# Placing every operation of a fused attention and feed-forward kernel with a list scheduler, and moving its turns from TensorE to the DMA crossbar

## The chip, the cores and the metric

The kernel runs on one core of a Trainium2 chip. The metric is the device time of one execution in microseconds (us), measured on the chip. Lower is better. The kernel before takes 428.44 us (median of 2 runs, 428.42 to 428.45).

Names used below: PE is TensorE (matmuls), DVE is VectorE, ACT is ScalarE, POOL is GpSimd, and SP is SyncE, which here only starts DMAs. PSUM is the memory that TensorE writes. To "turn" a tile means to transpose it. A "crossbar DMA" is this document's name for what the traces call DMA_TRANSPOSE: a DMA that transposes on its way.

## The reference

```python
# q, k, v: (8 batches, 8 heads, 576 rows, 64), float32; w_phi: (64, 128)
def phi(x):
    proj = einsum('bhsd,df->bhsf', x, w_phi)
    proj = proj - max(abs(proj), axis=-1, keepdims=True)      # row maximum
    return concatenate([exp(proj), exp(-proj)], axis=-1)
q_p, k_p = phi(q), phi(k)
kv  = einsum('bhsf,bhsd->bhfd', k_p, v)
z   = sum(k_p, axis=2)
num = einsum('bhsf,bhfd->bhsd', q_p, kv)
den = einsum('bhsf,bhf->bhs', q_p, z)[..., None] + 1e-06
x   = num / den                                               # -> (4608 tokens, 512)
out = (relu(x @ w_gate) * (x @ w_val)) @ w_out                # d_ff = 1536
```

Each batch passes through an attention stage (k features, the small matrices kv, q features, numerators and denominators) and then through a feed-forward stage. The feed-forward stage is most of the matmul work.

## The kernel before

Batches are handled as 512 rows in four blocks of 128, and the 64 rows left over are paired ("mixed" tiles). Operations are written by hand into time slots ("ticks"), and that order becomes the fixed order of each engine. k, q and x are turned by matmuls against an identity, and the result is copied from PSUM:

```python
def transposed(blocks):                       # k and q
    for i, blk in enumerate(blocks):
        nc.tensor.matmul(pt[:, P*i : P*i+P], lhsT=blk, rhs=ident, is_transpose=True)
    nc.vector.tensor_copy(t.rearrange("p a b -> p (a b)"), pt[:, 0 : n*P])

def project_rows(T2, m):                      # row-major projection + row maxima
    for i in range(2):
        nc.tensor.matmul(pp[:, 2*F*i : 2*F*(i+1)], lhsT=T2[:, i, :], rhs=w2...)
    nc.vector.tensor_reduce(m, pp..., axis=AX.X, op=ALU.max, apply_absolute_value=True)

def q_rows(st, i):                            # q: rows are projected for the maxima only
    project_rows(...); ...
    nc.scalar.activation(st["c"], st["m"], AF.Exp, scale=2.0)

def q_cols(st, x, slot, lo, par, first):      # q again, feature-major: the features used
    nc.tensor.matmul(pf, lhsT=w2[:, par, :], rhs=st["T"][:, lo : lo+4]...)
    nc.scalar.activation(x["qp"]..., pf, AF.Exp, scale=±1)

def q_finish(x, dst):                         # x is turned for the feed-forward
    for i in range(NDC):
        nc.tensor.matmul(pt[:, P*i : P*i+P], lhsT=x["xu"]..., rhs=ident, is_transpose=True)
    nc.vector.tensor_copy(dst, pt...)
# ... (numerators, feed-forward and the hand-written ticks are cut)
```

So q is projected twice: once row-major, to find the maxima, and once feature-major, to make the features. Most loads are on POOL; the loads of v from the third batch on are on SP, with the stores.

## Time and profile before

| | before |
|---|---|
| time, median | 428.44 us |
| span of the profiled run | 426.3 us |
| TensorE busy | 398.7 us (94%) |
| TensorE idle in the first 45 us / after that | 16.5 / 11.2 us |
| granted TensorE clock | 0.998 |

The lines below are from the page of the kernel before. The first gives busy time by engine; the others cut the span into 40 slices: each digit is a busy share in tenths, and PEclk is the TensorE clock that was granted, in tenths.

```profile
PE 398.7 (94%) x3357; PEld 232.9 (55%) x3416; DVE 284.1 (67%) x641; ACT 250.9 (59%) x575; POOL 159.6 (37%) x204
...
PE   3777899989999999999999999999999999999995
...
PEclk9999999999999999999999999999999999999999
DMA  8997795245413750167015901374020002002004
```

From the sixth slice to the last but one TensorE is full (9, once 8). The trace's records of the clock begin at 18.4 us and show the full clock until 424.6 us, after the last matmul. Before 18.4 us, 256-column projections start 214 ns apart, and 109 ns apart later: the start runs at about half speed, though the digits show it as 9. The next lines are the table by stretches of the same kernel; the columns are the stretch, its length, the busy us of each engine with its instruction count, the granted clock, the DMA share and GB/s.

```profile
core 0: us, PE busy (x) PEld busy (x) DVE busy (x) ACT busy (x) POOL busy (x), PEclk, DMA share, GB/s
90.00:135.00 45.00, 43.60 (x396) 26.06 (x402) 33.17 (x72) 30.10 (x71) 21.14 (x27) 1.00 0.38 74
135.00:180.00 45.00, 44.20 (x387) 26.12 (x395) 35.77 (x85) 28.57 (x66) 16.59 (x22) 1.00 0.41 74
...
270.00:315.00 45.00, 44.58 (x399) 26.41 (x405) 32.12 (x70) 30.80 (x73) 23.13 (x31) 1.00 0.40 80
```

In each 45 us of the middle TensorE is idle for 0.4 to 1.4 us. Nothing but less TensorE work, or a shorter start, can help much. Three groups of the same page show the work in question (line, engine, operation, output and input, count, busy us and mean ns, then the idle time before and its cause):

```profile
L147 DVE TENSOR_REDUCE mk<-pa 128x4 f32<-128x512 f32 x72 | 48.4, 682 | 11.3 <-PE pa L142 11.1
...
L299 PE MATMUL pa<-ident,xu 128*128 128x128 bf16 x144 | 14.0, 219 | 2.1 <-POOL xu L292 1.6
...
L305 DVE COPY xT<-pa 128x512 bf16<-128x512 bf16 x32 | 13.3, 417 | 1.9 <-PE pa L299 1.7
```

The reduction takes 682 ns, a turn of a 128x128 block of x 219 ns by its pipelined record. Last, the waits of SP's queue in the kernel before (total us, times, longest us):

```profile
SPq L355 <- ACT out_sb L352: 325.2, 31, 34.3
```

SP waits almost only for what it stores (this line, and 27.0 us at the last stores); 40 us more it stood before loads of v. Only stores and loads of v are on this queue.

### The profile page before, as it was taken

What the parts mean: (1) busy time and instruction counts of PE and PEld (TensorE: products, weight loads), DVE (VectorE), ACT (ScalarE), POOL (GpSimd) and SP (SyncE); (2) the same over time, 40 slices, a digit from 0 to 9 for tenths busy, and PEclk for the clock granted to TensorE, in tenths of its full rate; (3) what the DMA queues carried; (4) which work ended last, traced back from release to release, by engine and by line L of the source; (5) the groups of instructions that cost most, each with busy time, mean ns of one, the idle gap of its engine ahead of it and who ended that gap; (6) DMA issues with size and microseconds to landing.
All of it is one profiled execution on the core that took longest, in us unless ns stands there. A gap on an engine that the chain in (4) does not pass through costs nothing.

```text
span 426.3 us, 8695 instructions
## 1 busy us (share of the span) xinstructions
PE 398.7 (94%) x3357; PEld 232.9 (55%) x3416; DVE 284.1 (67%) x641; ACT 250.9 (59%) x575; POOL 159.6 (37%) x204
## 2 busy tenths in 40 slices
PE   3777899989999999999999999999999999999995
PEld 1556665645556556555566556555565554444442
DVE  4888569867687679866876699676856795330420
ACT  3984776566667755687567665766667552322321
POOL 8953861176217501574155211870362021000000
PEclk9999999999999999999999999999999999999999
DMA  8997795245413750167015901374020002002004
GB/s 157 199 265 164 108 181 61 75 122 59 56 51 98 128 61 2 61 156 94 2 59 160 116 3 52 71 139 51 26 76 2 1 14 86 2 0 100 0 2 98
DMA packets 45337, 33.66 MB, mean 79 GB/s; under 512 B 12848, under 2 KB 40112, under 8 KB 45296
## 3 DMA queue, kind: packets, MB, share of 16 engines
q0 software_dynamic: 30480, 16.52, 28.1%
q1 hardware_dynamic: 14816, 16.58, 12.4%
q8 instruction: 27, 0.44, 0.4%
q14 instruction: 14, 0.11, 0.1%
HBM read 37.81 MB, written 9.44 MB: 111 GB/s over the span
## 4 chain that ended last, share of the span: by engine, by line
PE 78%; DVE 10%; ACT 4%; POOL 2%; issue 2%; DMA 2%; POOLq 0%; DVEq 0%; ACTq 0%
PE pf L320 40%; PE pf L342 17%; PE pa L142 6%; PE pa L218 5%; PE pa L263 4%; PE pa L241 3%; PE pa L131 3%; DVE u L287 2%; DVE mk L147 2%; DMA qn_117<-in_q_dram 2%; DVE t L279 2%; PE pa L299 1%; POOL xu L292 1%; ACT qp L247 1%; ACT t L275 1%
## 5 line engine op out<-in xcount | busy, mean ns | idle before, releaser
L320 PE MATMUL pf<-xT,wv_sb 128*128 128x512 bf16 (+1 forms) x386 | 96.9, 366 | 3.8 <-DVE xT L305 2.6
L320 PE MATMUL pf<-xT,wg_sb 128*128 128x512 bf16 (+1 forms) x394 | 97.7, 366 | 2.0 <-ACT val_sb L329 1.4
L292 POOL TENSOR_TENSOR xu<-u,r 128x512 bf16<-128x512 f32 x36 | 37.5, 1042 | 164.1 <-DVE r L290 128.9
L329 ACT CAST val_sb<-pf 128x512 bf16<-128x512 f32 (+1 forms) x114 | 65.3, 573 | 52.7 <-PE pf L320 52.3
L247 ACT ACTIVATE qp<-pa 128x512 bf16<-128x512 f32 x128 | 69.5, 604 | 11.9 <-PE pa L241 11.9
L320 PEld LDWEIGHTS <-wg_sb 128*128 128x128 bf16 x456 | 44.4, 98 | 41.6 <-issue 2.1
L320 PEld LDWEIGHTS <-wv_sb 128*128 128x128 bf16 x456 | 43.3, 98 | 36.5 <-issue 3.9
L147 DVE TENSOR_REDUCE mk<-pa 128x4 f32<-128x512 f32 x72 | 48.4, 682 | 11.3 <-PE pa L142 11.1
L263 PEld LDWEIGHTS <-qp 128*128 128x128 bf16 x640 | 33.9, 98 | 21.5 <-issue 0.9
L287 DVE TENSOR_TENSOR u<-pa,t 128x195 f32<-128x195 f32 (+3 forms) x120 | 40.5, 338 | 6.8 <-ACT t L275 0.5
L279 DVE TENSOR_TENSOR t<-pa,cq 128x195 f32<-128x195 f32 (+3 forms) x114 | 37.6, 330 | 4.6 <-PE pa L263 3.8
L352 ACT COPY out_sb<-pf 128x512 f32<-128x512 f32 x36 | 21.3, 592 | 32.4 <-PE pf L342 29.5
L263 PE MATMUL pa<-kv,qp 128*128 128x65 bf16 x640 | 37.9, 193 | 0.9 <-DVE u L287 0.5
L331 DVE SCALAR_TENSOR_TENSOR h_6277<-pf,val_sb 128x512 bf16<-128x512 f32 x12 | 8.3, 692 | 22.8 <-PE pf L320 22.8
L331 DVE SCALAR_TENSOR_TENSOR h_6056<-pf,val_sb 128x512 bf16<-128x512 f32 x12 | 8.3, 692 | 14.5 <-PE pf L320 14.5
L299 PEld LDWEIGHTS <-xu 128*128 128x128 bf16 x144 | 10.7, 98 | 11.7 <-POOL xu L292 3.8
L223 ACT CAST kv<-pa 128x260 bf16<-128x260 f32 x28 | 10.7, 380 | 10.0 <-PE pa L218 9.9
L299 PE MATMUL pa<-ident,xu 128*128 128x128 bf16 x144 | 14.0, 219 | 2.1 <-POOL xu L292 1.6
L331 DVE SCALAR_TENSOR_TENSOR h_566<-pf,val_sb 128x256 bf16<-128x256 f32 (+1 forms) x18 | 9.1, 506 | 8.8 <-ACT val_sb L329 4.1
L331 DVE SCALAR_TENSOR_TENSOR h_1578<-pf,val_sb 128x512 bf16<-128x512 f32 x12 | 8.3, 691 | 9.6 <-ACT val_sb L329 5.7
L305 DVE COPY xT<-pa 128x512 bf16<-128x512 bf16 x32 | 13.3, 417 | 1.9 <-PE pa L299 1.7
L331 DVE SCALAR_TENSOR_TENSOR h_3132<-pf,val_sb 128x512 bf16<-128x512 f32 x12 | 8.2, 686 | 7.3 <-PE pf L320 3.8
(580 smaller groups left out, 776.1 us busy)
## 6 DMA issues: line engine op xcount, KB each, us to landing
out_dram<-out_sb SPq DMA_DIRECT2D x32, 256.0 KB, 2.3
wv_sb<-in_moe_w_val_dram POOLq DMA_DIRECT2D x3, 512.0 KB, 8.2
wg_sb<-in_moe_w_gate_dram POOLq DMA_DIRECT2D x3, 512.0 KB, 9.7
wo_sb<-in_moe_w_out_dram POOLq DMA_DIRECT2D x1, 1536.0 KB, 13.3
vn_1018<-in_v_dram SPq DMA_DIRECT2D x1, 1024.0 KB, 8.9
vn_335<-in_v_dram POOLq DMA_DIRECT2D x1, 1024.0 KB, 13.5
vn_1793<-in_v_dram SPq DMA_DIRECT2D x1, 1024.0 KB, 7.1
vn_2508<-in_v_dram SPq DMA_DIRECT2D x1, 1024.0 KB, 7.2
```

What stands on the lines that cost most here:

```text
L142: nc.tensor.matmul(pp[:, 2 * F * i : 2 * F * (i + 1)], lhsT=T2[:, i, :], rhs=w2.rearrange("p a f -> p (a f)"),)
L147: nc.vector.tensor_reduce(m, pp.rearrange("p (c f) -> p c f", f=F), axis=AX.X, op=ALU.max, apply_absolute_value=True,)
L247: nc.scalar.activation(x["qp"][:, s, slot].rearrange("p a b -> p (a b)"), pf, AF.Exp, scale=sign)
L263: nc.tensor.matmul(pn[:, E * (2 * i + s) : E * (2 * i + s + 1)], lhsT=x["qp"][:, s, slot, blk, :], rhs=kvs[b, h // 2][:, h % 2, s, :],)
L279: nc.vector.tensor_tensor(t, ab[:, :, 1], st["c"][rows, col(lo) : col(lo + n - 1) + 1 : col(1) - col(0)][:, :, None].to_broadcast([np_, n, ...
L287: nc.vector.tensor_tensor(x["u"][rows, lo : lo + n], ab[:, :, 0], t, op=ALU.add)
L292: nc.gpsimd.tensor_tensor(x["xu"], x["u"][:, :, 0:D], r.to_broadcast([P, 8, D]), op=ALU.mult)
L299: nc.tensor.matmul(pt[:, P * i : P * i + P], lhsT=x["xu"][:, 2 * i : 2 * i + 2].rearrange("p a d -> p (a d)"), rhs=ident, is_transpose=True,)
L320: nc.tensor.matmul(ps, lhsT=w[:, dc, P * fi : P * fi + P], rhs=xT[:, dc, lo:hi], start=(dc == 0), stop=(dc == NDC - 1),)
L329: nc.scalar.copy(st["val"], ps)
L331: nc.vector.scalar_tensor_tensor(st["h2"][:, fi, lo:hi], ps, 0.0, st["val"], op0=ALU.max, op1=ALU.mult)
L342: nc.tensor.matmul(st["po"], lhsT=st["h2"][:, fi, P * t : P * t + P], rhs=wo_sb[:, fi, :], start=(fi == 0), stop=(fi == NFC - 1),)
```

## The change

The intent is to take the turns and q's row-wise projection off the busiest engine:

1. Every operation becomes an object with an engine, an estimated duration, its dependences and its buffers. A list scheduler simulates the engines at build time and takes the ready operation with the smallest key. The resulting order is fixed in the program.
2. After the first batch, k, q and x are turned by crossbar DMAs, all issued by SP.
3. q's row maxima come from the feature-major projections. A transposing reduction gives the maxima of 32x32 blocks; one DMA carries these to DRAM, four DMAs bring them back in another arrangement, and a small reduction finishes ("the trip" below). There are seven such trips, one for each batch after the first, and four smaller ones for the mixed tiles: 11 trips, 55 DMAs. The row-wise projection of q goes.
4. The loads of v move from SP to ACT's queue.

The core of the diff (cut; the scheduler, the buffers and the feed-forward are left out):

```diff
-    def transposed(blocks):
-        ... nc.tensor.matmul(..., rhs=ident, is_transpose=True) ... nc.vector.tensor_copy(...)
+    def turn_dma(src, dst, nbytes, dst_buf, deps, key, src_buf):
+        def go():
+            nc.sync.dma_start_transpose(out=dst(), in_=src())
+        return op(SP, 0.1, go, deps, [src_buf, dst_buf], key=key, kind="a", nbytes=nbytes * 1.6)
...
-    def q_rows(st, i):
-        project_rows(...)
+        def amax():                                    # in q_cols
+            nc.vector.tensor_reduce(dst, ps.t.rearrange("p (h j t) -> p h j t", j=NQ, t=32),
+                axis=AX.X, op=ALU.max, apply_absolute_value=True, apply_transpose=True)
...
+    def q_scale(mq, mg, cq, n, deps, key):             # deps: all eight reductions of a batch
+        def away():
+            nc.sync.dma_start(out=dq.t[:, 0 : NQ * n], in_=mq.t...)        # to DRAM
+        def back():
+            for j in range(NQ):
+                nc.sync.dma_start(out=mg.t[32 * j : 32 * (j + 1)], in_=src[j])
+        def amax(): nc.vector.tensor_reduce(mc.t[:, 0:n], mg.t..., axis=AX.X, op=ALU.max)
+        def ex():   nc.scalar.activation(cq.t, mc.t[:, 0:n], AF.Exp, scale=2.0)
+        a  = op(SP, 0.1, away, deps, [mq, dq], ..., nbytes=P * NQ * n * 4)
+        b_ = op(SP, 0.4, back, [a], [mg, dq], ..., nbytes=P * NQ * n * 16)
...
-        at(t + 20, load_v, b + 1)                      # on SP
+        heads_of(b, "vn", v, nc.scalar, ACT, 0, H, (1, b), [o])
+        got["vm", b] = load_rest_by_head(b, v, nc.scalar, ACT, (1, b), ins[b]["vm"], [o])
...
-    for _, _, fn, args in sorted(events, key=lambda e: e[:2]):
-        fn(*args)
+    order = plan.run(lambda kind, now: 5 if kind == "a" else 4)
+    for o, e in order: ...
```

## The prediction

> **What bounds the kernel now.** TensorE. The page's busy line gives PE 398.7 us of a 426.3 us span (94%), DVE 67%, ACT 59%; the chain of waits is 78% PE. The table by stretches shows PE idle for 16.5 us of the first 45 us, 2.2 us from 45 to 90, 0.4 to 1.4 us in each later 45 us, and 4.9 us in the last 66. The granted clock is 0.99 to 1.00. So only fewer PE instructions, or a shorter start, can pay.
>
> **What goes.** Costs read start to start in the PE timeline (181 to 225 us): a 128x128 turn 56 ns, a 256-column projection 109 ns, a 512-column matmul 216 ns. By the instruction lists:
> - 254 of 288 turns of k and q go (batch 0 keeps its own): 14.2 us.
> - 128 of 144 row-wise projections of q, which served only the row maximum: 14.0 us.
> - 128 of 144 turns of x: 7.2 us.
>
> Sum 35.4 us. The feed-forward has 48 more matmuls but the same columns: about nothing. The same costs summed over all that before issues give 391 us; the other 35 us of its span are idle, cold clock and tails.
>
> **What moves.** DVE loses the copies of turned blocks (16 of 0.69 us, 76 of 0.42 us, a few kept) and gains 23 kv copies (0.43 us), 40 small reciprocals (0.2 us) and 11 small maxima. The 64 transposing reductions read the same 128x512 from PSUM; I estimate the 0.68 us of those they replace. DVE ends near 260 us, ACT near 230. Neither binds.
>
> **What is added.** 71 crossbar DMAs, about 12 MB, in SP's order with the stores. [...] This trace shows no such transpose; it is my weakest input. Each turned tile becomes a chain (POOL product, some 2 to 4 us of DMA, then PE), and q's maxima go through DRAM and back. These latencies lie beside an earlier batch's feed-forward and should mostly be hidden. But the order is fixed at build time: where a DMA lands later than the scheduler assumed, PE waits. I allow 1 us a batch.
>
> **On the critical path.** Nearly all 35.4 us, since PE has almost no idle after 45 us. Batch 0 keeps its PE turns and loads, so the start stays about as long; perhaps 5 us is won by filling it better. 428.4 - 35.4 - 5 + 7 = 395, and the scheduler may keep a little more.
>
> **Predicted: 393 us, 8 in 10 within 381 to 408. Chances: faster by over 2% 0.92, within 2% 0.04, slower 0.04.**
>
> **What would show each step.** PE busy near 363 us; turns gone from the PE groups after batch 0. PE idle after 45 us of 5 to 12 us, mainly released by DMAs on turned tiles. Transposing reduction 0.65 to 0.75 us. Crossbar DMAs of 256 KB landing in 3 to 5 us, mean DMA share 50 to 60%. First 45 us with 11 to 17 us of PE idle.
>
> **What would make it wrong.** Crossbar transposes several times slower (10 us per 256 KB would queue on SP and starve PE: no gain); a transposing reduction of twice the cost, making DVE the limit; SP holding a turn behind a waiting store; or, the other way, a much shorter start, giving under 381.

The mean DMA share of 50 to 60%: before, the queues' shares on the page add up to 41%, and what was to come on top was the estimate; 57% was measured. The times of 2 to 4 us and 3 to 5 us for crossbar DMAs are estimates too, and so are the 10 us per 256 KB; the trace before holds no crossbar DMA (its plain stores of 256 KB landed in 2.3 us, median), and what the kernel after measured is given below: 2.5 us for x's turns of 128 KB, 3.9 us for q's of 256 KB and 8.5 us for k's of 256 KB (medians). The "cold clock" is the start told of above (214 ns against 109 ns).

## More of the kernel before

One more thing matters later: the row maximum of q scales the numerator and the denominator of a row alike, so it cancels except against the 1e-06. It is there to follow the reference and to keep the exponentials in range.

## The result, and the profile after

The changed kernel takes 469.5 us (median of 2 runs, 469.23 to 469.76). Its ratio to the kernel before is 1.096, with a 95% interval of 1.093 to 1.099: it is slower by about 41 us, where 35 us of gain were expected. A ratio is the mean time of one kernel's fast runs over that of the other's in the same rounds, so it is not quite the ratio of the medians quoted.

The page after, the same lines:

```profile
PE 385.3 (82%) x2954; PEld 210.5 (45%) x2954; DVE 261.1 (56%) x644; ACT 237.6 (51%) x503; POOL 155.1 (33%) x179
...
PE   1769599659819594999997799989595999999995
...
PEclk9998899959969798799999899999797999999999
DMA  9999969530981929232097995406946003101004
```

The table by stretches after, the same rows:

```profile
90.00:135.00 45.00, 29.08 (x208) 14.86 (x207) 25.30 (x56) 21.75 (x48) 16.14 (x19) 0.84 0.64 99
135.00:180.00 45.00, 36.79 (x320) 20.13 (x320) 25.05 (x64) 26.79 (x57) 19.03 (x22) 0.85 0.52 86
...
270.00:315.00 45.00, 43.71 (x362) 23.50 (x361) 30.73 (x79) 27.19 (x57) 13.01 (x16) 1.00 0.51 100
```

TensorE is busy for only 29.1 us of the stretch from 90 to 135, and in that stretch its clock is 0.84. Where it isn't starved (270 to 315) it runs as before. So there are two losses. To size them I added up the records of the trace: the union of TensorE's busy intervals, and the part of it that lies in stretches at half clock. Half of the latter is lost, by arithmetic; "work" is the busy time less that half.

| us, profiled run | before | after |
|---|---|---|
| span | 426.3 | 467.3 |
| work at full clock | 398.7 | 364.7 |
| lost at half clock | 0 | 20.5 (half of 41.1) |
| idle, first 45 us | 16.5 | 18.6 |
| idle, later | 11.2 | 63.4 |

The saving of work came as intended (34.0 us). It was eaten by 52 us more of idle time and by 20.5 us of half clock, which before did not have at all in its clock records. (Those begin at 18.4 us before and at 18.6 us after. Busy time that lies earlier, 9.9 and 7.9 us, stands in the table as work, although in both kernels 256-column projections start 213 to 214 ns apart there, about half speed; by these numbers the difference between the kernels is an estimated 1 us.)

The same half clock can be read from single lines, in the chosen stretch of TensorE's timeline after (start, us, engine and line, operation, count, idle before it and its releaser):

```profile
124.05 1.03 PE L719 MATMUL ps<-xT,wv_sb 128*128 128x512 bf16 x4
...
138.15 0.38 PE L521 MATMUL ps<-vs,kp 128*128 128x65 bf16 x4 [11.86 <-ACT qp L567]
...
139.22 1.90 PE L719 MATMUL ps<-xT,wg_sb 128*128 128x512 bf16 x4
```

Four 512-column matmuls take 1.03 us before the gap of 11.86 us and 1.90 us after it. The trace's records of the clock hold 11 stretches at 0.5; they last 3.41, 6.83 or 10.24 us, multiples of 3.41 us (the last one runs past the end). I cut the trace into windows of that length, in step with the clock's changes. The 11 drops follow windows in which TensorE was busy for 0 to 44%; from the first record on, in the windows that kept the full clock it was busy for 48% or more, and the clock came back after windows in which it was busy for 79% or more. So in this trace several short gaps did what one long gap did: in the window before the drop at 158.6 us TensorE was busy for 29%, and no gap was over 1.5 us.

What was TensorE waiting for? The label of the gap says ACT. ACT's timeline in the same stretch:

```profile
121.85 0.38 ACTq L324 DMA_DIRECT2D vn<-in_v_dram  x1
122.35 14.13 ACTq L337 DMA_DIRECT2D vm<-in_v_dram  x2
136.53 2.56 ACT L567 ACTIVATE qp<-ps 128x512 bf16<-128x512 f32 x5 [14.19 <-DMA kT<-kn]
```

ACT did nothing for 14 us: it stood in the issue of the second half of a load ("vm", 64 KB of v), and the features that TensorE needed were behind that issue in ACT's order. SP's timeline in the same stretch:

```profile
121.97 5.35 SPq L397 DMA_TRANSPOSE kT<-kn  x2
127.42 0.53 SPq L583 DMA_DIRECT2D dq<-mq  x1
128.12 1.20 SPq L397 DMA_TRANSPOSE kmT<-km  x1
136.01 1.73 SPq L588 DMA_DIRECT2D mg<-dq  x4
```

SP started two turns of k at 121.97, then sent the maxima of q ("dq") at 127.42, and could issue the way back ("mg") only at 136.01. The out-leg of 64 KB needed 8.6 us beside k's turns.

Why did ACT stand in a load, which needs nothing from SP? The trace's DMA records name the semaphore that each DMA counts up and waits on. The 193 DMAs of SP and ACT share eight such semaphores in rotation, and each of them was issued only after the previous DMA on its semaphore had landed, at the closest 0.08 us after. The held load was started at 135.86; the previous DMA on its semaphore was a turn of k that landed at 135.79. The three other long holds of ACT have the same form, after a turn of k, a DMA of "mg" and one of "dq", each within 0.1 us of that landing. In the whole trace none of the 242 DMAs starts before the previous one on its semaphore has landed. Before, ACT issued no DMA, and no DMA waited in this way (each started at least 3.6 us after the previous one on its semaphore had landed). ACT's holds sum to 33.8 us after.

In this trace it is the issuing engine that stands in such a wait: ACT stood for 12.9 us before the load that was started at 135.86.

The waits of SP's queue after:

```profile
SPq L397 <- POOL xu L678: 76.8, 19, 14.1
SPq L397 <- DMA kn<-in_k_dram: 54.8, 5, 20.5
SPq L583 <- DVE mq L553: 37.6, 3, 18.6
...
SPq L588 <- DMA dq<-mq: 18.7, 6, 6.6
```

SP's order now holds urgent things behind waiting ones. It stood 37.6 us at the door of the trip until q's reductions were done, and 18.7 us until the out-leg had landed; turns and stores stood behind. The two larger waits, of turns for their own inputs, aren't what the trip costs: in e20 below, without the trip, they are 94.8 and 76.7 us. The DMA issues after (KB each where given, median us to landing):

```profile
out_dram<-ob SPq DMA_DIRECT2D x32, 256.0 KB, 2.4
...
dq<-mq SPq DMA_DIRECT2D x7, 64.0 KB, 3.0
mg<-dq SPq DMA_DIRECT2D x28, 16.0 KB, 2.1
xT<-xu SPq DMA_TRANSPOSE x28, 2.5
...
kT<-kn SPq DMA_TRANSPOSE x14, 8.5
qT<-qn SPq DMA_TRANSPOSE x14, 3.9
```

A turn of 256 KB of k takes 8.5 us, a store of the same 256 KB 2.4 us. From the end of the last reduction of a batch to the start of the small final one, the seven trips took 12.1, 19.2, 21.3, 9.4, 6.5, 13.5 and 5.8 us.

Three groups of the page after:

```profile
L719 PE MATMUL ps<-xT,wv_sb 128*128 128x512 bf16 (+1 forms) x432 | 103.7, 377 | 18.5 <-DMA xT<-xu 14.6
...
L567 ACT ACTIVATE qp<-ps 128x512 bf16<-128x512 f32 x144 | 77.3, 613 | 38.3 <-DMA kT<-kn 23.1
...
L553 DVE TRANSPOSE_TENSOR_REDUCE mq<-ps 128x16 f32<-128x512 f32 x56 | 37.7, 693 | 11.0 <-PE ps L546 10.1
```

The transposing reduction costs 693 ns, as the reduction it replaces. The idle times before the other two groups name turned tiles, x's and k's, as the releasers; for the second of them that name hides the hold of ACT described above (14.2 of the 23.1 us).

### The profile page after: what moved, and what is told of

It is laid out like the page before. It is cut to its first block, busy times and chain, and to the rows that moved or that the text cites. A ratio compares the mean times of both kernels' runs of the same rounds, so it can differ in the third digit from the quotient of the medians.

```text
span 467.3 us, 8066 instructions
## 1 busy us (share of the span) xinstructions
PE 385.3 (82%) x2954; PEld 210.5 (45%) x2954; DVE 261.1 (56%) x644; ACT 237.6 (51%) x503; POOL 155.1 (33%) x179
## 5 line engine op out<-in xcount | busy, mean ns | idle before, releaser
L728 DVE SCALAR_TENSOR_TENSOR h<-ps,val 128x512 bf16<-128x512 f32 (+1 forms) x120 | 75.4, 631 | 95.5 <-PE ps L719 85.9
L719 PE MATMUL ps<-xT,wv_sb 128*128 128x512 bf16 (+1 forms) x432 | 103.7, 377 | 18.5 <-DMA xT<-xu 14.6
L719 PE MATMUL ps<-xT,wg_sb 128*128 128x512 bf16 (+1 forms) x432 | 102.4, 373 | 7.2 <-ACT qp L567 7.2
L678 POOL TENSOR_TENSOR xu<-u,r 128x512 bf16<-128x512 f32 x36 | 37.6, 1043 | 210.4 <-issue 134.0
L725 ACT CAST val<-ps 128x512 bf16<-128x512 f32 (+1 forms) x120 | 65.1, 545 | 82.9 <-PE ps L719 81.7
L749 PE MATMUL ps<-wo_sb,h 128*128 128x512 bf16 x432 | 102.5, 382 | 0.0
L567 ACT ACTIVATE qp<-ps 128x512 bf16<-128x512 f32 x144 | 77.3, 613 | 38.3 <-DMA kT<-kn 23.1
L407 ACT ACTIVATE kp<-ps 128x512 bf16<-128x512 f32 x128 | 69.0, 633 | 6.0 <-PE ps L431 4.0
L454 POOL TENSOR_TENSOR vs<-vn,ek 128x1024 bf16<-128x1024 f32 x30 | 57.1, 1904 | 40.0 <-DVE ek L417 25.3
L749 PEld LDWEIGHTS <-h 128*128 128x128 bf16 x432 | 40.6, 98 | 43.6 <-issue 2.2
L759 ACT COPY ob<-ps 128x512 f32<-128x512 f32 x32 | 18.7, 585 | 64.4 <-PE ps L749 59.7
L438 DVE TENSOR_REDUCE mk<-ps 128x4 f32<-128x512 f32 x64 | 40.9, 675 | 12.9 <-PE ps L431 10.4
L650 PEld LDWEIGHTS <-qp 128*128 128x128 bf16 x640 | 30.9, 101 | 25.5 <-issue 11.2
L521 PE MATMUL ps<-vs,kp 128*128 128x65 bf16 x512 | 22.6, 195 | 11.9 <-ACT qp L567 11.9
```

The lines of the kernel that those rows point to most:

```text
L407: nc.scalar.activation(dst(s), ps.t[:, 0:n], AF.Exp, scale=sign)
L438: nc.vector.tensor_reduce(m.t[:, C * hh : C * (hh + 1)], ps.t.rearrange("p (c f) -> p c f", f=F), axis=AX.X, op=ALU.max, apply_absolute_va ...
L454: eng.tensor_tensor(vs.t[:, :, :, 0:D], vn.t[:, 2 * u : 2 * u + 2].rearrange("p h c d -> p (h c) d")[:, :, None, :] .to_broadcast([P, 2 * ...
L521: nc.tensor.matmul(acc[:, hh, s, :], lhsT=lhsT, rhs=rhs, start=(n == 0), stop=(n == 19))
L567: nc.scalar.activation(dst(s), ps.t.rearrange("p (h b) -> p h b", b=P), AF.Exp, scale=sign)
L650: nc.tensor.matmul(ps.t[:, E * (2 * i + s) : E * (2 * i + s + 1)], lhsT=qp.t[:, s, h, :], rhs=kv_of[b][h // 2][0].t[:, h % 2, s, :],)
```

## The experiments

The theories at the start: (1) ACT is held in the loads of v, which the change put on its queue; (2) the trip of q's maxima through DRAM delays the numerators; (3) k's and q's crossbar turns land late; (4) the list's estimates of DMA times are wrong (for a 256 KB turn 0.1 us of SP, where the trace has 1.2 us or more; and a landing that by the list's constants comes some 3.4 us after the start where no other load is planned beside it, where the trace has 8.5 us); (5) the order of the list itself is worse than the ticks. Eighteen kernels were run (no kernel e15 or e16 is on record), all of them with a result that passed the comparison. Each was timed in three rounds beside the kernel before, which took 428.6 to 429.1 us. Beside e13, e14 and e17 one run of the kernel before took 851 us, and beside e18 and e19 one took 439 us; both are left out as slow. Medians and ranges below are of all four runs of a kernel; e1, e6, e7, e8 and e11 had one slow run each, the upper end of the range, and the ratios are of fast runs alone. The kernels ran on several chips, so two of them are best compared by their ratios to the kernel before. Some matmul records are missing from the traces (43 in e20, some 80 in the kernel before); by the short holes that they leave, an estimate, this adds 2 and 3 us to the idle times of these two.

A caution for all kernels with a changed operation: the list plans anew, so the order changes with it. Four kernels keep the order of the changed kernel: e1, e5 and e6, which change nothing but a queue, and e20. Likewise e8 keeps the order of e3, and e11 that of e10.

### e1: the loads of v on POOL's queue

```diff
-        heads_of(b, "vn", v, nc.scalar, ACT, ...)
+        heads_of(b, "vn", v, nc.gpsimd, ACT, ...)      # planned as before, issued by POOL
```

> Only the queue of the 21 loads of v for batches 1 to 7 changes, from ScalarE's to GpSimd's; the order of PE, DVE, SP and of ScalarE's own work is the same. Theory 1 (ScalarE is held inside its own DMA issues: in the trace the second small v load of batch 3 issues 13.5 us after the first, of batch 4 8.8 us, batch 5 8.1 us, batch 7 7.3 us, each ending with a TensorE gap of 11.9, 7.2, 1.8 and 4.9 us): those four gaps go, the half-clock stretches after them too; 467 becomes 425 to 445. Theory 2 (turned tiles and q's maxima land late, whoever issues v): the gaps stay under other names; 460 to 470.

Measured: 454.6 us (451.1 to 461.0), ratio 1.058. ACT's holds fell from 33.8 us to none, and TensorE's later idle time from 63.4 to 48.4 us. That lies between the two ranges. Theory 1 is worth some 15 us of the 76 us between the prediction and the result, and isn't the main cause.

### e2: the list scheduler alone

All turns on TensorE, the maxima by rows, as before; only the order is the list's.

```diff
-        if first:            # turns of k; likewise q, x and the maxima by rows
+        if first or K_PE:    # K_PE, Q_PE, X_PE, Q_ROWS = True, True, True, True
```

> The list scheduler alone: k, q and x turned by TensorE and q's maxima from row-wise projections, for all batches. v is still issued from ScalarE. TensorE work goes up by 35 us over the changed kernel, to that of before. Theory 1: no crossbar DMA is there to hold ScalarE's issues, so no gap over 4 us after 45 us: 420 to 435. Theory 2: no late turned tile or maximum, the same 420 to 435. Theory 3 (the fixed order of the list itself is bad, whatever turns the tiles): TensorE idle stays over 60 us and the time over 470.

Measured: 421.5 us (420.5 to 422.9), ratio 0.984. Theory 5 falls in this form: the list alone gains 1.6%. Its later idle time is 5.2 us, less than the 11.2 us of the ticks. Whether the list orders the DMAs of the change well is another question, to which e20 returns.

### e3: crossbar turns, but the maxima by rows (no trip)

```diff
+K_PE, Q_PE, X_PE, Q_ROWS = False, False, False, True
```

> Only q's maxima go back to row-wise projections (14 us more TensorE work); k, q, x still turned by crossbar, v still from ScalarE; the list is planned anew. If the maxima's way through DRAM is the cause, TensorE idle drops by 25 us or more and the time to 440 to 450. Theory 1: ScalarE is still held in its v issues while crossbar DMAs fly: 465 to 480.

Measured: 424.3 us (422.5 to 426.8), ratio 0.990. Although it does 12 us more TensorE work than the changed kernel (376.5 against 364.7), it is 45 us faster, below both ranges. It still has 7.5 us of ACT's holds.

### e4: the trip, but k and q turned by TensorE

```diff
+K_PE, Q_PE, X_PE, Q_ROWS = True, True, False, False
```

> Only k and q are turned by TensorE again (14 us more TensorE work), x by crossbar, maxima by round trip; planned anew. If the 256 KB crossbar DMAs are what holds ScalarE (theory 1) or what lands late (theory 2), both say 425 to 445; if x's turns or the maxima are the cause, it stays above 460.

Measured: 423.6 us (422.6 to 426.9), ratio 0.990. Again 46 us come back, and the time is just below the first range. So most of the damage needs both the trip and the turns of k and q. But e4 isn't free of it: against e2, 17 us less TensorE work (378.6 against 395.6) came with 15 us more of later idle time (20.6 against 5.2), and the time is no better. What part of this is the trip's, and what part x's crossbar turns', isn't shown. In e4 SP sent the maxima as soon as the reductions had ended (up to 6.1 us later in the changed kernel), and the seven trips took 5.4 to 9.9 us. The out-leg alone was no faster in the median (3.5 us, against 3.0).

### e5, e6: the trip on POOL's queue, alone and with the loads of v

```diff
-            nc.sync.dma_start(out=dq.t...), nc.sync.dma_start(out=mg.t...)
+            nc.gpsimd.dma_start(out=dq.t...), nc.gpsimd.dma_start(out=mg.t...)
```

> Only the queue of the DMAs that carry q's maxima to DRAM and back changes, from SP's to GpSimd's; the order of every other instruction is the same, v stays on ScalarE's queue. In the changed kernel the way from the last transposing reduction of a batch to the maximum that uses it took 12.1, 19.2, 21.3, 9.4, 6.5, 13.5 and 5.8 us; in batches 1 to 3, 4.8 to 6.1 us of it passed before the first DMA was even issued, because SP stood at k's crossbar turns. If the place behind k's turns on SP is the cause, the way is under 9 us in every batch and the time 425 to 445. If the contention of the 16 engines or the held ScalarE is the cause, the way stays over 12 us in batches 2, 3 and 6 and the time over 455.

> Both queue changes together: v (as e1) and the maxima's way (as e5) on GpSimd's queue, SP left with turns and stores. If the two are separate causes, their gains add to at least 35 us: under 430, TensorE idle after 45 us under 30 us. If slow crossbar DMAs themselves are the cause (k's land after 8 to 16 us wherever the others are issued), it stays over 440.

Measured: 445.7 us (444.8 to 449.6) and 446.9 us (444.8 to 452.5), ratios 1.041 and 1.040. e5 meets neither theory: it ends just above 445 us, with trips of 9 us or more in six of seven batches. e6 is over 440 us, as the theory of slow crossbar DMAs had it. The gains of e1 (15 us) and e5 (24 us) don't add up; taking the trip off SP also freed ACT (1.2 us of holds); in the trace of the changed kernel POOL's 49 DMAs count on eight semaphores of their own, which neither SP nor ACT uses. But 41 us of later idle time stay. In e5 the trips still took 6.6 to 14.0 us, though the out-leg was issued 0.3 us after the last reduction each time: it landed after 2.2 to 9.8 us. So the place behind k's turns on SP is only a part of the trip's length.

### e7: x turned by TensorE

```diff
+K_PE, Q_PE, X_PE, Q_ROWS = False, False, True, False
```

> Only x is turned by TensorE again (7 us more TensorE work), k and q by crossbar, maxima by round trip on SP, v from ScalarE; planned anew. x's 128 KB turns landed in 2.5 us at the median and ended 14 us of TensorE waits. If they were a main cause, the time drops to 440 or less; if k's turns with the round trip are, it stays at 455 to 475.

Measured: 458.5 us (456.1 to 465.4), ratio 1.067. That is 11 us less than the changed kernel, although TensorE does 6 us more work (371.1 us). The time is in the range of the other theory, so x's turns aren't the main part. How much of the 11 us is theirs isn't shown: in the new order ACT's holds fell as well, from 33.8 to some 16 us.

### e8: e3 with the loads of v on POOL

> No round trip (as e3) and v on GpSimd's queue (order of e3 otherwise). e3 kept 7.5 us of held issues on ScalarE (5.6 us of it before its largest gap, 3.8 us). If that holding is real and separate, 412 to 420 against 424 of e3; if not, the same within 2 us.

Measured: 420.6 us (418.6 to 425.0), ratio 0.979; the run that was profiled was its slow one. It is 4 us faster than e3 by the medians, from another chip, just short of the range for a separate effect (ratios 0.979 and 0.990).

### e9: the same operations, with measured DMA times in the list

The store's time in the list (0.1 to 0.5 us of SP) and one more dependence of the feed-forward, on the gate weights, changed as well; both are left out of the cut.

```diff
-        return op(SP, 0.1, go, ..., nbytes=nbytes * 1.6)       # a turn
+        return op(SP, 1.25, go, ..., nbytes=nbytes * 4.0)
-        a  = op(SP, 0.1, away, ...);  b_ = op(SP, 0.4, back, ..., nbytes=P * NQ * n * 16)
+        a  = op(SP, 0.5, away, ...);  b_ = op(SP, 1.75, back, ..., nbytes=P * NQ * n * 4)
```

> The changed kernel with the same operations, but the list planned with DMA times read from the trace: 1.25 us of SP per crossbar DMA instead of 0.1, a 256 KB turn taking 3 us of the engines instead of 1.2, 0.5 us of SP per store and 1.75 us for the four DMAs back (and no feed-forward pair started before both weight slices are there, without which that plan sticks). Theory A (the fixed order was built on too short times): 415 to 440. Theory B (with such times the chain of q, columns to maxima through DRAM to numerators to x, is itself too long for the four buffers of q's features, in any order): no better than 455.

Measured: 453.3 us (452.0 to 458.0), ratio 1.061. The holds of ACT go (0.9 us), 16 us come back, and 42 us of later idle time stay. The time lies between the two ranges. Theory 4, as the main cause, falls.

### e10: no trip, and measured times

> No round trip (as e3) and planned with the measured DMA times (as e9); v still from ScalarE. Theory A: the wrong times cost e3 too, its 16.5 us of TensorE idle after 45 us and 19 us at half clock shrink: 400 to 415. Theory B says the round trip was the trouble and the times matter little without it: 418 to 426, as e3.

Measured: 411.5 us (408.0 to 412.9), ratio 0.959 (0.954 to 0.963). This is the fastest correct version, faster than both kernels. The measured times win 13 us here too (424.3 us in e3), as Theory A had it. TensorE's later idle time is 9.9 us, its half-clock loss 5.1 us, and its work 372.4 us.

### e11, e12: e10 with v on POOL, and the same with x turned by TensorE

In e12 the loads of v are also planned on POOL, so e11 is its neighbour, not e10.

> e10 with v's loads on GpSimd's queue at the same places of the list. If ScalarE is still held in issues in e10, some us faster than e10 (398 to 412); if e10 has none of those holds, the same within 2 us.

> No round trip, measured times, v planned on GpSimd's queue, x turned by TensorE (7 us more TensorE work than e11), only k and q by crossbar. If x's crossbar turns, the last step before each feed-forward, still end waits of TensorE, it beats e11; if they are hidden, it is 5 to 7 us slower than e11.

Measured: 415.2 us (413.7 to 420.9), ratio 0.967; and 420.1 us (415.9 to 421.9), ratio 0.978. Neither improves on e10. In e10 ACT isn't held in its loads (0.4 us), so there was nothing to gain from moving them; e11 is even 4 us slower, outside the 2 us that were expected. e12 is 5 us slower than e11 for 5 us more TensorE work: x's crossbar turns pay for themselves.

### e13, e19: only the DMAs of the trip taken away

So far "no trip" meant "maxima by rows", which changes the work too. These two keep every projection and every transposing reduction, and take away only the five DMAs of each trip. The small last reduction reads the columns that never left, so the maxima are wrong. The outputs still agree with the reference within its tolerance, because the maximum cancels between numerator and denominator. These kernels are tests and no candidates.

```diff
-        a  = op(SP, ..., away, deps, [mq, dq], ...)
-        b_ = op(SP, ..., back, [a], [mg, dq], ...)
-        r = op(DVE, ..., amax, [b_], [mg, mc], ...)      # reads mg
+        r = op(DVE, ..., amax, deps, [mq, mc], ...)      # reads mq
```

> Wrong result on purpose. The kernel with measured DMA times in its list (453 us) with the three DMAs of q's maxima taken out: the reduction of the maxima reads the columns that never left. The transposing reductions and the feature-major projections stay. Theory B1 (what costs is the latency of these DMAs): 400 to 420 us, TensorE idle after 45 us under 15 us. Theory B2 (what costs is that all numerators wait for all eight column reductions, with or without DMAs): 435 us or more.

(The text counts three DMAs; they are five, one out and four back.) Measured for e13, with measured times: 402.8 us (400.4 to 404.3), ratio 0.939. Against e9 this is 50 us.

> Wrong maxima on purpose. The changed kernel itself (469.5 us, its own times in the list) with only the DMAs of q's maxima taken out, replanned. If these DMAs are the main cause in the changed kernel too: 410 to 430 us, the holds of ACT in its own issues under 10 us and TensorE's idle time after 45 us under 20 us. If they matter only once the times in the list are right: 440 us or more.

Measured for e19, the changed kernel itself with its own times: 406.0 us (404.3 to 407.1), ratio 0.946. Against the changed kernel this is 63.5 us, for 55 small DMAs. The page of e19, and its rows of the table by stretches:

```profile
PE 370.9 (92%) x2954; PEld 207.9 (51%) x2954; DVE 265.5 (66%) x649; ACT 234.8 (58%) x498; POOL 155.1 (38%) x179
...
PE   0775959996999999999999999999999999999995
...
PEclk9968869998999999999999999999999999999998
```

```profile
90.00:135.00 45.00, 41.47 (x343) 22.79 (x342) 36.56 (x91) 29.89 (x65) 21.94 (x25) 0.96 0.73 119
135.00:180.00 45.00, 43.77 (x362) 23.43 (x361) 35.51 (x90) 31.00 (x65) 21.85 (x26) 1.00 0.78 145
...
270.00:315.00 45.00, 45.00 (x373) 24.34 (x372) 35.64 (x96) 29.75 (x62) 20.29 (x22) 1.00 0.60 98
```

TensorE is full again (41.5 to 45.0 us in these stretches), and its clock is back (0.96 to 1.00). Span by span, from the changed kernel to e19: later idle time from 63.4 to 14.2 us, half-clock loss from 20.5 to 9.8 us, work from 364.7 to 361.0 us; ACT's holds from 33.8 to 0.8 us. The time is even below its range. In e19 the loads of v and the turns of k still overlap in every batch (k's turns land in 7.1 us, median), but with 55 DMAs fewer ACT's holds are down to the 0.8 us. The theory that it is the dependence of the numerators on all eight reductions falls as the main cause, since e13 and e19 both keep it.

### e20: the changed kernel's own order, without the trip's DMAs

e19 was planned anew, so its gain holds both the trip's absence and a different order. e20 keeps the plan of the changed kernel, with the trip in it, and merely doesn't issue the trip's DMAs; the last small reduction reads the columns that never left (maxima wrong, output within the tolerance as in e19). The order on the other engines is the changed kernel's.

```diff
         def away():
-            nc.sync.dma_start(out=dq.t[:, 0 : NQ * n], in_=mq.t...)
+            pass
         def back():
-            for j in range(NQ):
-                nc.sync.dma_start(out=mg.t[32 * j : 32 * (j + 1)], in_=src[j])
+            pass
         def amax():
-            nc.vector.tensor_reduce(mc.t[:, 0:n], mg.t..., axis=AX.X, op=ALU.max)
+            nc.vector.tensor_reduce(mc.t[:, 0:n], mq.t..., axis=AX.X, op=ALU.max)
```

> The changed kernel with exactly its own plan, so that every engine keeps its order, in which the five DMAs of each trip are simply not issued and the last small reduction reads the columns that never left (maxima wrong on purpose). If the landing of the trip, its waits on SP and the semaphores it takes are the cause, in the given order: 405 to 425 us. If a good part of e19's 63 us came from the better order that the list found without the trip: 430 to 450 us. If the order is nearly all of it: over 455 us.

Measured: 428.5 us (426.5 to 431.5), ratio 1.000 (0.994 to 1.005): between the first two ranges. So of the 63.5 us of e19, 41 us come from the trip itself in the given order, and 22.6 us (428.5 against 406.0) from the better order that the list finds without it. The page of e20:

```profile
PE 373.4 (88%) x2911; PEld 207.2 (49%) x2954; DVE 261.3 (61%) x644; ACT 237.3 (56%) x503; POOL 155.2 (36%) x179
...
PE   1676589949998699999996999999959998999995
...
PEclk9988999988999699999998999999979999999998
```

ACT's holds are gone (1.2 us), the later idle time fell from 63.4 to 34.2 us and the half-clock loss from 20.5 to 12.3 us. Of the 34 us that stay, 20 go with the order: e19, with the same estimates of DMA times but an order of its own, has 14.2 us. One mark of that order can be seen: the small last reduction stands 4.5 to 11.4 us behind the last of the eight in e20, though no DMA lies between them, and at most 0.5 us behind in e19. The list had put other work into the time that it gave to the trip.

### e14: the loads of v held back until k's turns have landed

```diff
+        if b > 1:
+            for o in (got["vn", b, 0], got["vm", b]):
+                o.deps.append(turned_k[H - 1])
```

> The changed kernel with the loads of v (batches 2 and later) made dependent on k's turns, so that in the list they are issued after them. Theory C (k's turns land late, 8 us, because loads run beside them): k's median landing falls to 3 to 5 us and the time to 425 to 450 us. Theory B (the waits on the round trip of q's maxima and the in-order queues): the landing may fall but the time stays within 2% of 469 us, since the loads then come later for their own consumers.

Measured: 451.7 us (450.1 to 453.0), ratio 1.053. The turns of k in e14:

```profile
kT<-kn SPq DMA_TRANSPOSE x14, 4.0
```

They land in 4.0 us (median) instead of 8.5: the lateness was contention with the loads of v, now shown. The time fell by 18 us, just short of the contention theory's range, and beyond what the other theory allowed. ACT's holds fell as well, to 18.8 us, so not all of it is due to the faster landing. Contention is a part; 47 us of later idle time stay.

### e17: the trip added to the fastest version

The maxima by rows go out to DRAM and come back unchanged, two DMAs for each group; the result is right.

```diff
+        a_ = op(SP, 0.5, away, reds, [mq, dq], ...)
+        b_ = op(SP, 0.5, back, [a_], [dq, mback], ...)
-        return cq, op(ACT, 0.27, ex, reds, [mq, cq], ...)
+        return cq, op(ACT, 0.27, ex, [b_], [mback, cq], ...)
```

> The fastest version (maxima by rows, measured times, 411.5 us) with one thing added: each batch's row maxima go out to DRAM and come back unchanged before they are used, two small DMAs on SP. The result stays right. Theory B1 (the latency of a trip through DRAM between q's maxima and its numerators is what costs): 430 to 455 us, with TensorE idle after 45 us of 30 us or more. Theory B2 or C (the trip itself is hidden, something else of the transposing form costs): 408 to 420 us.

Measured: 447.7 us (446.4 to 449.3), ratio 1.043. Against e10 this is 36 us, and TensorE's later idle time goes from 9.9 to 31.4 us. About half of it is the first batch, which has no trip in the changed kernel: there one gap of 18.9 us stands at 30 to 49 us. The waits that name the trip in e17, and those of SP's queue:

```profile
ACT cr L643 <- DMA mb<-dq: 28.7, 4, 18.7
DVE t L701 <- ACT cr L643: 28.3, 5, 18.4
...
PE ps L549 <- DVE u L708: 18.9, 1, 18.9
```

```profile
SPq L634 <- DVE mr L622: 36.8, 12, 16.7
...
SPq L637 <- DMA dq<-mr: 26.9, 13, 8.1
```

The scale of q waited 28.7 us for the trip to land, the multiplication by it as long again, and TensorE 18.9 us behind that. SP stood 36.8 us at the start of trips and 26.9 us in the middle of them. Most of the first two waits is that gap of the first batch (18.7 and 18.4 us). So e17 shows that the trip slows a good kernel too, but by about half of its 36 us in a place where the changed kernel has no trip.

### e18: the list told that the trip is long

```diff
-        a = ..., nbytes=P * NQ * n * 4);  b_ = ..., nbytes=P * NQ * n * 4)
+        a = ..., nbytes=862500);          b_ = ..., nbytes=862500)        # 2.5 us more each
```

> The kernel with measured DMA times in its list (453 us), in which the list is now told that each of the two legs of the trip of q's maxima takes 2.5 us more (about 12 us in all, the mean of the trace, instead of about 7). No instruction is added or removed. If the list could hide the trip once it knows its length: 405 to 425 us, like the version without it. If the trip can't be hidden with these buffers and this order: 440 us or more.

Measured: 490.7 us (489.4 to 493.5), ratio 1.145, with the very same instructions as e9.

The list didn't hide the trip; it made the trips longer (12.7 to 20.0 us, against 5.9 to 15.5 in e9) and the kernel 37 us slower than e9. In three of the seven trips the DMAs had landed 8.1 to 10.2 us before the small last reduction ran, so there its place in DVE's order held it, not the DMAs. ACT's holds were back too (some 23 us). Two numbers in the list move this kernel by 8%. Whether a different rule (the trip of one batch under the features of another, more buffers for q's features) could hide it stays open: none of these lists did.

## Why the prediction was wrong

Point by point, in the terms of the prediction's own sum (428.4 − 35.4 − 5 + 7):

- **Less TensorE work, 35.4 us.** Right: 34.0 us (398.7 to 364.7 at full clock).
- **Transposing reduction, 0.65 to 0.75 us; DVE near 260, ACT near 230.** Right: 0.693 us, 261.1 and 237.6 us.
- **Mean DMA share, 50 to 60%.** Measured: 57%, the sum of the queues' shares on the page.
- **A start shorter by 5 us.** Wrong, but small: the idle time in the first 45 us grew by 2.1 us.
- **"Crossbar DMAs of 256 KB landing in 3 to 5 us."** Wrong for k beside the loads: 8.5 us (median); right for q (3.9 us), for k at its best (3.1 us), and for k in e14 (4.0 us).
- **"These latencies lie beside an earlier batch's feed-forward and should mostly be hidden … I allow 1 us a batch."** This is the step that failed. The allowance was 7 us in all; the later idle time rose by 52.2 us. e19 shows which latency: with only the trip's DMAs gone, the idle time is 14.2 us, close to the 5 to 12 us predicted, and the kernel takes 406.0 us, within the range that was given for the whole change. So the turns of k, q and x could be hidden nearly as predicted, and the trip couldn't. e20 shows that 41 us of the 63.5 are the trip's in the very same order.
- **The clock.** Missing from the prediction. The clock dropped 11 times, each time after a window of 3.41 us in which TensorE was busy for 44% or less, and 41.1 us of TensorE's busy time ran at half speed, a loss of 20.5 us.

Added up in the profiled runs: −34.0 of work, +2.1 at the start, +52.2 later, +20.5 of half clock, together +40.8 of the 41.0 us between the spans.

What the runs show in place of the failed step: the trip made SP stop up to twice in a batch, once for the reductions and once for its own out-leg, with turns of k, q and x behind it in SP's fixed order; it lay between q's reductions and the numerators, a way of 6 to 21 us (of which 4.5 to 11.4 us stay in e20, where the order alone makes them); and it put 55 more DMAs on the eight semaphores that SP and ACT share, so that ACT stood in loads of v until turns of k (two of the four long holds) or DMAs of the trip (the other two) had landed. That the trip's DMAs are the cause is shown by e20 (41 us in the same order); e13, e19 and, in the other direction, e17 agree, each with an order of its own. That the semaphores hold ACT is shown by the trace (four holds, each ended within 0.1 us of the landing); e1, which takes that away, wins 15 us. The trip does most of its harm together with the crossbar turns of k and q: without those (e4) it takes less time itself (5.4 to 9.9 us), and no turn of k or q stands behind it on SP.

What stays open: the 41 us that e20 wins back in the given order are not divided further with certainty. e1 (15 us) and e5 (24 us) take away parts of them, but these parts overlap, and each also changed where other DMAs wait. Nor is it shown what makes the list's order with the trip worse by 22.6 us than its order without it; that the last reduction stands late in it, seen in e20, is one property, and what it costs wasn't tested. e18 only shows that telling the list a longer trip doesn't mend this.

Among the ways to be wrong, the prediction named turns of "10 us per 256 KB", which came close for k beside loads, and "SP holding a turn behind a waiting store". The first isn't the cause: in e13 and e19 k's turns still land in 8.3 and 7.1 us (medians), and both kernels are fast. For the second, SP did hold turns, but behind the trip; its waits at the stores of the batches (32.2 us) are even longer in the fast e19 (57.6 us).

## What to carry to other kernels

Before you move work from the busiest engine to DMAs, draw the chain that the DMAs make and ask what stands behind each of its waits in the fixed order of the engine that issues them: here legs that landed in 2 to 3 us (medians) became a way of 6 to 21 us, because they had to wait for compute, held a queue, and lay between two steps of one batch. Keep a round trip through DRAM out of the middle of a batch, even at the price of redundant matmuls: here keeping the row-wise projection of q costs 8 to 12 us of TensorE work (372.4 in e10 and 376.5 in e3, against 364.7 us), and the kernel with it, planned with measured DMA times, is 42 us faster than the same list with the trip (411.5 against 453.3). And when the limit is TensorE, count more than the gaps themselves, where the traces show the clock falling with them: here 54 us more of idle time came with 20.5 us of half clock.

## What the traces show of the DMAs and the clock

- A turn of 256 KB of k landed after 3.1 us at best and 8.5 us in the median, most of them beside loads; loads of v held back brought the median to 4.0 us (e14).
- A plain store of 256 KB landed in 2.1 us at best and a turn of k of the same size in 3.1 us at best (medians 2.4 and 8.5 us), in one trace. The two weren't measured under the same load, so this alone doesn't show that a turn is slower.
- Moving the small DMAs of the trip from SP to POOL saved 24 us (e5), and v's loads on ACT's queue held ACT for 33.8 us: the order of waits on a queue counts.
- DMAs issued by SP and by ACT shared completion semaphores in rotation, so that one engine's issue waited for another's DMA: 193 DMAs shared eight, with four holds of 4.9 to 12.9 us.
- A crossbar DMA of 64 to 256 KB held its issuing engine for 1.2 to 1.5 us (medians), and up to 6.1 us, against 0.4 to 0.5 us (medians) for the trip's plain DMAs.
- The clock was not in the sum of the prediction, and half clock cost 20.5 us. In the changed kernel it dropped after windows of 3.41 us in which TensorE was busy for up to 44%, and stayed full from 48% on. Where this border lies in general isn't shown.
